# A scale's product moved to the end of its slot, and a second first product taken into the attention's last steps

## The chip, the cores and the metric

The kernel runs on one core of a Trainium2 chip. The metric is the device time of one execution in microseconds (us). Before the change three runs gave 850.76, 851.49 and 851.49 us, median 851.49 us. The rows below come from one further execution that was profiled: 851.16 us, of which the span from the first to the last instruction is 849.2 us.

## The reference

Three independent computations, all in one launch; the products have to be nearly as exact as float32.

```python
# 1: attention, 4 batches x 8 heads, 576 tokens, head size 64; heads 0-3 see a band of 32, heads 4-7 every 32nd token
attn = softmax(where(mask, q @ k.T / 8, -1e9)) @ v
# 2: x (2304 x 512), w_in (512 x 2048), w_out (2048 x 512)
h = x @ w_in
out = (h * cos(h)) @ w_out
# 3: w_gate and w_val (512 x 1536), w_out2 (1536 x 512)
out = (silu(x @ w_gate) * (x @ w_val)) @ w_out2
```

In the kernel the three are chained: the attention's output is the tokens x of the second part, whose output is the tokens of the third.

## The kernel before

**Number format.** A weight or token matrix is multiplied with a power of two (its scale, from its greatest absolute value) and split into two float16 parts: the high part on ScalarE (L272), the low part on VectorE (L275). A product of one chunk is three matmuls, high by high, high by low, low by high (L593, L594, L595). One unit of 512 tokens by 128 columns of the hidden layer is 12 matmuls of 128x512.

**Making a scale.** VectorE finds row maxima of a matrix (L201 for weights as they come from HBM, L571 for tokens), then `spread_tops` reduces them to one number for each partition (L125, then L128 and L130 or L133). `common_scale` brings that number to all partitions by a small matmul on TensorE (L140; one for each scale, up to three) and takes the maximum on VectorE (L142), followed by three tiny instructions (L117 to L119). Only then can the splits that use the scale run.

**Stages.** The attention comes first: 48 groups of scores that go through a pipeline of several steps (k = 0 to 55), with `put` (L548, L557, on ScalarE) writing the result to the token buffer at the end. In the last eight steps no new group starts. Then comes the second part in 5 blocks of tokens (512, 512, 512, 384, 384), each with 16 slots. Slot m of a block makes product m (`up1`, the 12 matmuls), and then an evaluation of h·cos(h) that is spread over this and the next slots: `up1_a` on ScalarE (L626), `up1_b` on VectorE (L629), the sine `up1_c` on ScalarE (L633; its first use loads ScalarE's function table), `up1_d` on VectorE (L636), and `up1_e` on ScalarE and GpSimd (L640, L641). The contraction with w_out (`down1`, again 12 matmuls of L593 to L595, into `acc`) runs from slot 16 on, one or two in a slot. The third part follows (L747 among its lines).

**What sets the order.** Each engine runs its instructions in the order of the program. One slot issues: the product and contractions, `up1_a` of this slot, `up1_b` of the slot before, `up1_d` and `up1_e` of earlier ones, one piece of the list `urgent` (`pump_urgent`: maxima, tops, scales and splits of the next block's tokens), and pieces of the list of weight work (`pump`: loads, maxima, splits; as many as a budget of time allows) before and after `up1_c`.

**Attention's last steps.** Where a step has no new group, TensorE gets one filler matmul of 128x384 (`keep_warm`, L827), except in two of them (k = 49, 50), where the first product of block 0 runs instead, half of its 12 matmuls in each (`EARLY = 1`). Its `up1_a` is issued in the second. The main loop then starts at slot 1. The accumulators `acc` of the main loop get the PSUM banks that the attention held, so they wait for its last `put`.

Of the kernel before, what the change touches and what calls it, by code (L numbers as in the profile page):

```python
# [30 lines left out]
LW = 64 + STRIDE  # L31
# [10 lines left out]
TX = 2.0 ** 10  # L42
# [8 lines left out]
WARM = 8  # L51
PUMP, KP = 1.05, 8
XSAT = 12
EARLY, K0 = 1, 1
HEAD, HSHARE = 16, 0.8
RATE, MINLAG = 0.7, 2
ALONE = 4
# [23 lines left out]
def build(tc, qk_l, qk_s, v_l, v_s, w_in, w_out, w_gate, w_val, w_out2, out):  # L81
    nc = tc.nc
    wide = w_in.dtype != F32
    with ExitStack() as ctx:
# [12 lines left out]
        id16 = small.tile([128, 128], BF16, name="id16")  # L97
# [359 lines left out]
        def bank():  # L457
            return pm.tile([128, 512], F32, name="bank")
# [103 lines left out]
        def scale_pieces(blks, scales, at_once=1):  # L562
            n = len(blks)
            parts = cols("parts", n * (KC + 1)).rearrange("p (n k) -> p n k", n=n)
            box = {}
            nc.gpsimd.memset(parts[:, :, KC:], TINY)
            todo = [(i, k) for i in range(n) for k in range(KC)]

            def piece(some):
                for i, k in some:  # L570
                    nc.vector.tensor_reduce(out=parts[:, i, k:k + 1], in_=xy[blks[i]][:, k, :], op=ALU.max, axis=AX.X,  # L571
                                            apply_absolute_value=True)
            for i in range(0, len(todo), at_once):
                yield 0.65 * at_once, lambda some=todo[i:i + at_once]: piece(some)
            yield 0.6, lambda: box.__setitem__("top", spread_tops(parts if n > 1 else parts[:, 0], False, n))
            yield 0.6, lambda: scales.update(zip(blks, common_scale(box["top"], TX, n)))

        def split_pieces(blk, scales, dst):
            n = BLOCKS[blk][1]
# [43 lines left out]
        def up1_a(c):  # L623
            n = c["n"]
            c["w"] = ring.tile([128, 512], F32, name="tb", bufs=4)[:, 0:n]
            nc.scalar.activation(out=c["w"].bitcast(I32), in_=c["ph"], func=AF.Identity, scale=turn[c["blk"]], bias=quarter)  # L626
# [195 lines left out]

        steps = deque()

        def keep_warm():
            t = bank()[:, 0:4 * LW].rearrange("p (n w) -> p n w", w=LW)
            nc.tensor.matmul(out=t, lhsT=id16, rhs=ml, start=True, stop=True)  # L827

        for k in range(len(gs) + LAGS[3] + 1):
            def group(lag):  # L830
                return gs[k - lag] if 0 <= k - lag < len(gs) else None
            i, g = 2 * (k // 6), k % 6
            if group(LAGS[0]):
                group(LAGS[0]).sums()
            if group(LAGS[1]):
                group(LAGS[1]).transposes()
            if group(0):
                group(0).scores()
                group(0).top()
            begun = k - len(gs) - K0  # L840
            if 0 <= begun < 2 * EARLY:
                m = begun // 2
                if begun % 2 == 0:
                    need(("in", m))
                    early = up1(0, m, range(KC // 2))
                else:
                    up1(0, m, range(KC // 2, KC), early)
                    steps.append((0, m, early))
            elif not group(0):
                keep_warm()  # L850
            if group(LAGS[3]):
                group(LAGS[3]).put()
            if group(LAGS[1]):
                group(LAGS[1]).evac()
            if group(LAGS[2]):
                group(LAGS[2]).values()
            if group(0) and g == 5:
                for j in (i + 2, i + 3):
                    if i and j < len(units):
                        load_v(j)  # L860
                for j in (i + 6, i + 7):
                    if j < len(units):
                        load_qk(j)
            if group(1):
                group(1).exps()
            if group(0):
                pump(PUMP if k >= KP else 0)
            if group(LAGS[0]):
                group(LAGS[0]).norm()
            if not group(0):  # L870
                if 0 <= begun < 2 * EARLY and begun % 2:
                    up1_a(early)
                pump(PUMP if k >= KP else 0)
            if k >= RELEASE:
                release()
# [147 lines left out]
        def urge(pieces, key=None):  # L1023
            urgent.extend((c, f, key) for c, f in pieces)

        def pump_urgent():
            if urgent:
                cost, fn, key = urgent.popleft()
                fn()
                emitted.add(key)  # L1030
                credit[0] -= cost
# [31 lines left out]
        for blk in range(NBLK):  # L1063
            for m in range(M1):
                n = BLOCKS[blk][1]
                if slot < EARLY:
                    slot += 1
                    continue
                if blk == 0:
                    need(("in", m))  # L1070
                if m == 0:
                    if blk:
                        need_urgent(("xs", blk))
                    if blk == NBLK - 1:
                        urge(fold_pieces(0, sy, ys, spans), ("ys", 0))
                if m == (2 if blk else XM) and blk + 1 < NBLK:
                    if blk == 0:
                        urge(scale_pieces([1], sx))
                    elif blk == 1:
                        urge(scale_pieces([2, 3, 4], sx, 2))  # L1080
                    urge(split_pieces(blk + 1, sx, xs), ("xs", blk + 1))
                if blk == NBLK - 2 and m == M1 // 2:
                    urge(scale_pieces([0], sy))
                if blk == NBLK - 1 and m == MINLAG + 2:
                    urge(scale_pieces([1, 2, 3], sy, 2))
                c = up1(blk, m, spare=slot // 2 % KC if slot % 2 and 1 < slot < HEAD - 4 else None)
                if blk == NBLK - 1 and m in (7, 14):
                    load_w7(m // 7 - 1)
                lag = 99 if slot < HEAD else max(MINLAG, HEAD - 2 - int((slot - HEAD) * RATE))
                work = 2.6 * n / 512  # L1090
                while len(queue) + 1 > lag:
                    work += down_next()
                if slot >= HEAD:
                    open_weights(lag)
                up1_a(c)
                up1_b(steps[-1][2])
                if len(steps) > 1:
                    up1_d(steps[-2][2])
                if len(steps) > 2:
                    finish(steps.popleft())  # L1100
                budget = (work - 1.25 * n / 512) * (HSHARE if slot < HEAD else SHARE if blk < SB else SHARE2)
                pump_urgent()
                pump(budget * 0.5)
                up1_c(steps[-1][2])
                pump(budget * 0.5)
                steps.append((blk, m, c))
                slot += 1
        up1_b(steps[2][2])
# [267 lines left out]
```

## Time and profile before

| what | value |
|---|---|
| median of three runs | 851.49 us |
| profiled execution | 851.16 us |
| its span | 849.2 us |
| TensorE busy | 841.6 us, 99% |
| VectorE busy | 650.9 us, 77% |
| ScalarE busy | 518.6 us, 61% |
| GpSimd busy | 203.1 us, 24% |
| granted TensorE clock | 1.00 |

TensorE is busy nearly all the time, so the end is set by the sum of its matmuls and of the few places where it waits. The other engines' shares are averages over stages; what matters is where one of them makes TensorE wait. The trace names at each instruction how long the engine was idle before it and what released it (in brackets). Matmuls overlap by their pipeline, so the spacing of two starts, not the duration, is what one costs.

### The profile page before, as it was taken

The page shows a single profiled execution, that of the slowest core. Times are in us where ns is not written, and L with a number is a line of the kernel's source. Part 1 is how long each engine was busy: PE and PEld are TensorE (multiplying, and loading weights), DVE is VectorE, ACT ScalarE, POOL GpSimd, SP SyncE. Part 2 cuts the span into 40 slices and gives each one's busy share as a digit, 9 for nine tenths or more (in the row PEclk, how much of TensorE's full clock was granted, in tenths as well). Part 3 has the DMA queues.
Part 4 walks back from the last instruction along what each step waited for, and adds up shares of the span by engine and source line. Part 5 has one row for each costly group of instructions (what it writes and reads, how often), then busy time and mean ns, then how long its engine had stood idle before and what let it go on. Part 6 is the DMA issues. An engine that isn't in the chain of part 4 may idle for free.

```text
span 849.2 us, 18347 instructions
## 1 busy us (share of the span) xinstructions
PE 841.6 (99%) x7225; PEld 601.0 (71%) x7225; DVE 650.9 (77%) x1256; ACT 518.6 (61%) x1047; POOL 203.1 (24%) x279
## 2 busy tenths in 40 slices
PE   9999999999999999999999999999999999999998
PEld 5677544444444444566666888888888899999998
DVE  7999988997889878799996388567756765665562
ACT  6899989555656767778985466545344444444440
POOL 5454344111445455422223001000000000000000
PEclk9999999999999999999999999999999999999999
DMA  9998812896556567415366247767777678788894
GB/s 366 408 351 304 291 62 97 304 335 252 197 199 230 194 210 223 163 49 184 113 217 237 81 183 285 249 220 263 235 252 251 231 269 293 283 304 318 323 325 162
DMA packets 53477, 201.99 MB, mean 238 GB/s; under 512 B 5264, under 2 KB 15760, under 8 KB 49552
## 3 DMA queue, kind: packets, MB, share of 16 engines
q1 hardware_dynamic: 53392, 200.84, 66.4%
q8 instruction: 56, 0.92, 0.4%
q14 instruction: 29, 0.24, 0.1%
HBM read 176.83 MB, written 23.99 MB: 236 GB/s over the span
## 4 chain that ended last, share of the span: by engine, by line
PE 81%; DVE 6%; DMA 5%; ACT 4%; POOL 1%; issue 1%; SPq 0%; ACTq 0%; POOLq 0%
PE acc L747 14%; PE bank L593 13%; PE bank L595 13%; PE bank L594 13%; PE acc L595 7%; PE acc L593 7%; PE acc L594 7%; DMA raw<-w_in 3%; PE po L535 2%; PE bank L478 2%; POOL arena L641 1%; DMA raw<-w_out 1%; ACT tb L626 1%; PE bank L747 1%; DMA raw<-w_val 1%
## 5 line engine op out<-in xcount | busy, mean ns | idle before, releaser
L593 PE MATMUL bank<-xs,wi 128*128 128x256 f16 (+3 forms) x780 | 232.6, 298 | 0.5 <-ACT cv L1244 0.5
L595 PE MATMUL bank<-xs,wi 128*128 128x256 f16 (+3 forms) x780 | 232.6, 298 | 0.0
L594 PE MATMUL bank<-xs,wi 128*128 128x256 f16 (+3 forms) x780 | 232.6, 298 | 0.0
L641 POOL TENSOR_TENSOR arena<-tb,arena 128x512 f16<-128x512 f32 (+1 forms) x80 | 89.9, 1125 | 235.3 <-ACT arena L640 202.1
L595 PE MATMUL acc<-arena 128*128 128x512 f16 (+1 forms) x320 | 114.5, 358 | 0.7 <-DVE arena L275 0.7
L593 PE MATMUL acc<-arena 128*128 128x512 f16 (+1 forms) x320 | 114.5, 358 | 0.0
L594 PE MATMUL acc<-arena 128*128 128x512 f16 (+1 forms) x320 | 114.5, 358 | 0.0
L594 PEld LDWEIGHTS <-wi 128*128 128x128 f16 x880 | 86.1, 98 | 35.8 <-issue 1.2
L593 PEld LDWEIGHTS <-wi 128*128 128x128 f16 x880 | 86.1, 98 | 34.8
L595 PEld LDWEIGHTS <-wi 128*128 128x128 f16 x880 | 86.1, 98 | 34.8
L747 PEld LDWEIGHTS <-arena 128*128 128x128 f16 x1080 | 100.8, 98 | 8.1
L731 POOL TENSOR_TENSOR wi<-tb 128x256 f32<-128x256 f32 (+1 forms) x30 | 20.2, 673 | 337.7 <-DVE tb L713 337.7
L1248 DVE TENSOR_TENSOR arena<-bank,cv 128x512 f32<-128x512 f32 (+1 forms) x60 | 37.9, 636 | 66.2 <-PE bank L595 66.2
L716 ACT ACTIVATE arena<-tb 128x256 f16<-128x256 f32 (+3 forms) x59 | 28.7, 486 | 97.1 <-DVE tb L713 90.1
L595 PEld LDWEIGHTS <-arena 128*128 128x128 f16 x600 | 58.7, 98 | 34.0 <-DVE arena L275 1.2
L594 PEld LDWEIGHTS <-arena 128*128 128x128 f16 x600 | 58.7, 98 | 32.7 <-issue 0.2
L593 PEld LDWEIGHTS <-arena 128*128 128x128 f16 x600 | 58.7, 98 | 32.4
L747 PE MATMUL acc<-arena 128*128 128x256 f16 (+1 forms) x684 | 80.2, 266 | 0.0
L640 ACT ACTIVATE arena<-tb 128x512 f16<-128x512 f32 (+1 forms) x80 | 46.6, 583 | 52.5 <-PE acc L595 50.9
L626 ACT ACTIVATE tb<-bank,quarter,c 128x512 int32<-128x512 f32 (+1 forms) x75 | 54.4, 725 | 28.9 <-PE bank L595 20.5
L713 DVE SCALAR_TENSOR_TENSOR tb<-tb,c,arena 128x512 f32<-128x512 f32 (+1 forms) x60 | 41.7, 695 | 34.4 <-ACT tb L708 34.4
L1244 ACT ACTIVATE cv<-bank 128x512 f32<-128x512 f32 (+1 forms) x90 | 49.2, 547 | 29.3 <-PE bank L595 28.4
(154 smaller groups left out, 1718.1 us busy)
## 6 DMA issues: line engine op xcount, KB each, us to landing
wi<-w SPq DMA_DIRECT2D x20, 1792.0 KB, 7.6
arena<-w SPq DMA_DIRECT2D x60, 576.0 KB, 4.8
raw<-w_out SPq DMA_DIRECT2D x56, 512.0 KB, 4.7
arena<-w SPq DMA_DIRECT2D x10, 1792.0 KB, 8.4
raw<-w_gate SPq DMA_DIRECT2D x24, 512.0 KB, 4.3
raw<-w_val SPq DMA_DIRECT2D x24, 512.0 KB, 5.6
w<-arena SPq DMA_DIRECT2D x42, 256.0 KB, 2.8
raw<-w_in SPq DMA_DIRECT2D x16, 512.0 KB, 9.1
```

The lines of the kernel that those rows point to most:

```text
L593: nc.tensor.matmul(out=o, lhsT=w[:, 0, c], rhs=x[0], start=first, stop=False, **kw)
L594: nc.tensor.matmul(out=o, lhsT=w[:, 0, c], rhs=x[1], start=False, stop=False, **kw)
L595: nc.tensor.matmul(out=o, lhsT=w[:, 1, c], rhs=x[0], start=False, stop=last, **kw)
L626: nc.scalar.activation(out=c["w"].bitcast(I32), in_=c["ph"], func=AF.Identity, scale=turn[c["blk"]], bias=quarter)
L640: nc.scalar.activation(out=g[:, 0, 0:n], in_=w, func=AF.Copy)
L641: nc.gpsimd.tensor_tensor(out=g[:, 1, 0:n], in0=w, in1=g[:, 0, 0:n], op=ALU.subtract)
L713: nc.vector.scalar_tensor_tensor(out=t, in0=t, scalar=s_g[c["blk"]], in1=c["C"][m][:, 1, 0:c["n"]], op0=ALU.mult, op1=ALU.mult)
L716: nc.scalar.activation(out=to, in_=src, func=AF.Copy, scale=2.0 ** -11)
L731: nc.gpsimd.tensor_tensor(out=t_sums[:, 0, 0:h], in0=c["t"][0][:, h:2 * h], in1=c["t"][0][:, 0:h], op=ALU.subtract)
L747: nc.tensor.matmul(out=o[:, c], lhsT=w[:, 256 * i + 128 * c:256 * i + 128 * c + 128], rhs=unit(u)[:, x:x + h], start=j == i == 0 and c == ...
L1244: nc.scalar.activation(out=t, in_=src, func=AF.Copy)
L1248: nc.vector.tensor_tensor(out=c["C"][m][:, :, h * right:h * right + h], in0=p, in1=t, op=ALU.add)
```

## The change

Two things change. `EARLY` goes from 1 to 2: the product of slot 1 of block 0 also runs in halves, at k = 51 and 52, in place of two fillers; so the fillers go from six to four, and the main loop starts at slot 2. With `up1_a` of product 1, in step 52, `up1_b` and `up1_c` of product 0 are issued too. The fillers share one PSUM bank. And the piece `common_scale` of a token scale carries a mark (`behind`): it isn't issued ahead of a slot's weight work any more, but at the slot's last place, and in the same slot as its `spread_tops`, where it used to come in the next slot. Since `up1_a`, `up1_b` and the product of that slot stand ahead, its L140 stands behind the slot's matmuls on TensorE.

```diff
-EARLY, K0 = 1, 1
+EARLY, K0 = 2, 1
...
-            yield 0.6, lambda: scales.update(zip(blks, common_scale(box["top"], TX, n)))
+
+            def spread():
+                scales.update(zip(blks, common_scale(box["top"], TX, n)))
+            spread.behind = True
+            yield 0.6, spread
...
+        warm = []
+
         def keep_warm():
-            t = bank()[:, 0:4 * LW].rearrange("p (n w) -> p n w", w=LW)
-            nc.tensor.matmul(out=t, lhsT=id16, rhs=ml, start=True, stop=True)
+            if not warm:
+                warm.append(bank()[:, 0:4 * LW].rearrange("p (n w) -> p n w", w=LW))
+            nc.tensor.matmul(out=warm[0], lhsT=id16, rhs=ml, start=True, stop=True)
...
                     up1(0, m, range(KC // 2, KC), early)
-                    steps.append((0, m, early))
...
                 if 0 <= begun < 2 * EARLY and begun % 2:
                     up1_a(early)
+                    if steps:
+                        up1_b(steps[-1][2])
+                        up1_c(steps[-1][2])
+                    steps.append((0, m, early))
...
-        def pump_urgent():
-            if urgent:
+        def pump_urgent(behind=None):
+            if urgent and behind in (None, hasattr(urgent[0][1], "behind")):
...
-                pump_urgent()
+                pump_urgent(False)
                 pump(budget * 0.5)
                 up1_c(steps[-1][2])
                 pump(budget * 0.5)
+                pump_urgent(True)
                 steps.append((blk, m, c))
```

Line numbers of the changed kernel are 4 greater from `project` on (L626 becomes L630, L629 L633, L633 L637, L636 L640).

The order of ScalarE's instructions at the end of the attention (`pt` is the last softmax block that is copied out; `xy` the token buffer that `put` writes; `wi` the parts of w_in). Before:

```order
L524 ACTIVATE pt<-tp 96x384
L272 ACTIVATE wi<-wi,s_1703 128x512
L557 ACTIVATE xy_69<-po 128x8x6
L557 ACTIVATE xy_70<-po 128x8x12
L272 ACTIVATE wi<-wi,s_1703 128x512
L548 ACTIVATE xy_70<-po 128x192
L272 ACTIVATE wi<-wi,s_1703 128x512 x2
L626 ACTIVATE tb<-bank,quarter,c_2021 128x512
L633 ACT_TABLE_LOAD
L633 ACTIVATE tb<-tb,right 128x512
```

Now:

```order
L524 ACTIVATE pt<-tp 96x384
L630 ACTIVATE tb<-bank,quarter,c_2021 128x512
L637 ACT_TABLE_LOAD
L637 ACTIVATE tb<-tb,right 128x512
L272 ACTIVATE wi<-wi,s_1703 128x512
L557 ACTIVATE xy_69<-po 128x8x6
L557 ACTIVATE xy_70<-po 128x8x12
L272 ACTIVATE wi<-wi,s_1703 128x512
L548 ACTIVATE xy_70<-po 128x192
L272 ACTIVATE wi<-wi,s_1703 128x512 x2
```

Product 1's `up1_a`, the table load and the first sine moved ahead of four high splits of w_in and of the attention's last two `put`s.

VectorE's order where the tokens of block 1 get their scale, in block 0 (`parts` are the row maxima of those tokens, `pw_out` those of w_out). Before:

```order
L125 TENSOR_REDUCE m_2316<-pw_out 128x1
L128 TENSOR_SCALAR a_2319<-m_2316 128x1
L130 SCALAR_TENSOR_TENSOR p_2317<-m_2316,a_2319 128x1
L629 SCALAR_TENSOR_TENSOR tb<-acc_2295,c_2021,tb 128x512
L636 SCALAR_TENSOR_TENSOR tb<-tb,bank 128x512
L125 TENSOR_REDUCE m_2341<-parts_2226 128x1
L133 TENSOR_SCALAR p_2342<-m_2341 128x1
L258 TENSOR_SCALAR cv<-cv 128x512
L629 SCALAR_TENSOR_TENSOR tb<-bank,c_2021,tb 128x512
L636 SCALAR_TENSOR_TENSOR tb<-tb,acc_2295 128x512
L142 TENSOR_REDUCE q_2371<-bank 128x1
```

Now:

```order
L633 SCALAR_TENSOR_TENSOR tb<-acc_2287,c_2021,tb 128x512
L640 SCALAR_TENSOR_TENSOR tb<-tb,bank 128x512
L125 TENSOR_REDUCE m_2327<-parts_2217 128x1
L133 TENSOR_SCALAR p_2328<-m_2327 128x1
L275 SCALAR_TENSOR_TENSOR wi<-wi,s_1703 128x512
L142 TENSOR_REDUCE q_2334<-bank 128x1
L117 RECIPROCAL s_2337<-q_2334 128x1
L118 TENSOR_SCALAR inv_2338<-q_2334 128x1
L119 TENSOR_SCALAR s_2337<-s_2337 128x1
```

The tokens' maximum (L142) moved up by a slot, to one instruction behind its top (L133), and ahead of w_out's top. On TensorE its L140 moved from behind product 9 to behind product 8.

The same in slot 24, where blocks 2 to 4 get theirs (`raw` holds rows of weights from HBM, `cv` a converted one, `arena` the parts of w_out). Before:

```order
L125 TENSOR_REDUCE m_3044<-parts_2620 128x3
L133 TENSOR_SCALAR p_3045<-m_3044 128x3
L201 TENSOR_REDUCE pw_two<-raw 128x1 x2
L258 TENSOR_SCALAR cv<-cv 128x512
L262 SCALAR_TENSOR_TENSOR cv<-raw,cv 128x512
L275 SCALAR_TENSOR_TENSOR arena<-cv,s_2408,arena 128x512
```

Now:

```order
L125 TENSOR_REDUCE m_3037<-parts_2607 128x3
L133 TENSOR_SCALAR p_3038<-m_3037 128x3
L142 TENSOR_REDUCE q_3043<-bank 128x3
L117 RECIPROCAL s_3048<-q_3043 128x3
L118 TENSOR_SCALAR inv_3049<-q_3043 128x3
L119 TENSOR_SCALAR s_3048<-s_3048 128x3
L201 TENSOR_REDUCE pw_two<-raw 128x1 x2
L258 TENSOR_SCALAR cv<-cv 128x512
L262 SCALAR_TENSOR_TENSOR cv<-raw,cv 128x512
L275 SCALAR_TENSOR_TENSOR arena<-cv,s_2469,arena 128x512
```

The four instructions of `common_scale` moved ahead of ten of weight work; on TensorE the three L140 moved from behind slot 25 to behind slot 24. In the same way the L140 of the first block's tokens of the third part moved from behind slot 61 to behind slot 60. The L140 of w_gate and w_val, whose piece has no mark, comes one slot later than before (behind product 27 instead of 26).

## Rows read from the trace of the kernel before

**Rows 1.** The page, busy time, share of the span and instructions.

```profile
PE 841.6 (99%) x7225; PEld 601.0 (71%) x7225; DVE 650.9 (77%) x1256; ACT 518.6 (61%) x1047; POOL 203.1 (24%) x279
```

**Rows 2.** TensorE's waits (engine, line, waited for: us, times, longest).

```profile
PE acc L595 <- DVE arena L275: 0.7, 1, 0.7
```

**Rows 3.** Timeline, TensorE, attention's end: start, us, line, out<-in, count [idle before].

```profile
93.80 0.38 PE L593 MATMUL bank<-xs,wi 128*128 128x512 f16 x1
...
95.19 0.68 PE L535 MATMUL po<-pts,v_pair 108*64 108x54 f32 x16
...
96.07 0.33 PE L827 MATMUL bank<-ml,id 128*128 128x384 bf16 x1
96.33 0.57 PE L535 MATMUL po<-pt,vl 96*64 96x64 f32 x12
...
97.19 0.33 PE L827 MATMUL bank<-ml,id 128*128 128x384 bf16 x1
...
99.04 0.38 PE L593 MATMUL bank<-xs,wi 128*128 128x512 f16 x1
...
104.22 0.38 PE L593 MATMUL acc<-xs,wi 128*128 128x512 f16 x1
```

**Rows 4.** Timeline, ScalarE, in the same stretch.

```profile
98.42 0.43 ACT L557 ACTIVATE xy<-po 128x48 f32<-128x48 f32 x2
98.64 0.73 ACT L272 ACTIVATE wi<-wi,s 128x512 f16<-128x512 f32 x1
99.25 0.34 ACT L548 ACTIVATE xy<-po 128x192 f32<-128x192 f32 x1
...
101.83 0.78 ACT L626 ACTIVATE tb<-bank,quarter,c 128x512 int32<-128x512 f32 x1 [0.51 <-PE bank L595]
102.63 1.28 ACT L633 ACT_TABLE_LOAD   x1
103.93 0.72 ACT L633 ACTIVATE tb<-tb,right 128x512 f32<-128x512 f32 x1
```

**Rows 5.** Timeline, VectorE, from there to the top of block 1's tokens.

```profile
98.56 0.75 DVE L275 SCALAR_TENSOR_TENSOR wi<-wi,s 128x512 f16<-128x512 f32 x1 [0.50 <-ACT wi L272]
...
120.30 0.15 DVE L133 TENSOR_SCALAR p<-m 128x1 int32<-128x1 int32 x1
```

**Rows 6.** Windows: busy time of each engine (instructions), clock, DMA share, GB/s.

```profile
98.56:120.45 21.89, 21.89 (x110) 10.01 (x107) 19.94 (x35) 17.49 (x29) 6.04 (x6) 1.00 0.48 174
```

**Rows 7.** Timeline, VectorE, slots 24 to 27.

```profile
194.07 1.26 DVE L201 TENSOR_REDUCE pw_two<-raw 128x1 f32<-128x512 f32 x2
...
196.31 0.74 DVE L275 SCALAR_TENSOR_TENSOR arena<-cv,s,arena 128x512 f16<-128x512 f32 x1
...
204.00 0.56 DVE L142 TENSOR_REDUCE q<-bank 128x3 f32<-128x384 f32 x1 [1.34 <-PE bank L140]
...
204.69 1.09 DVE L118 TENSOR_SCALAR inv<-q 128x3 f32<-128x3 f32 x1
...
212.97 0.15 DVE L118 TENSOR_SCALAR inv<-q 128x2 f32<-128x2 f32 x1
```

**Rows 8.** Timeline, GpSimd, beside VectorE's L118 of slot 26.

```profile
204.59 1.16 POOL L641 TENSOR_TENSOR arena<-tb,arena 128x512 f16<-128x512 f32 x1 [10.47 <-DVE q L142]
```

**Rows 9.** Timeline, TensorE, slots 25 to 27.

```profile
194.99 0.38 PE L593 MATMUL bank<-xs,wi 128*128 128x512 f16 x1
...
201.46 0.39 PE L595 MATMUL acc<-arena 128*128 128x512 f16 x1 [0.70 <-DVE arena L275]
...
203.63 0.33 PE L140 MATMUL bank<-id,p 128*128 128x128 bf16 x3
...
212.10 0.29 PE L140 MATMUL bank<-id,p 128*128 128x128 bf16 x2 [0.37 <-DVE p L130]
```

**Rows 10.** Timelines at the end of slot 60, TensorE and VectorE.

```profile
388.05 0.33 PE L593 MATMUL bank<-xs,wi 128*128 128x384 f16 x1
...
388.50 0.15 DVE L133 TENSOR_SCALAR p<-m 128x1 int32<-128x1 int32 x1
```

## The prediction

> **What bounds the kernel now.** I read the page first, then TensorE's waits, then the timelines of the places that the change touches. TensorE is busy 841.6 of 849.2 us [rows 1], and its matmuls stand back to back: from product 1 to product 3 there are 24 of them in 104.22 - 99.04 = 5.18 us, 0.216 each, 2.59 for a unit of twelve [rows 3]. The end therefore moves by what is added to or taken from TensorE's line, and by nothing else. Only two waits of the second part can be won back here. One is at 201.46, where a contraction waits for a low part of w_out from VectorE [rows 2, 9]: it is the 26th matmul after 194.99, so it was due at 200.60 and costs 0.87, of which the trace gives 0.70 as idle. The other is at 212.10, where L140 waits for the top of w_gate and w_val, 0.37 by the trace [rows 9]; with the same 0.17 that the idle time leaves out it costs 0.54. So the most that the change can give is these two and what the fillers cost. Against this stands every wait that it makes. VectorE is the engine to look at: it is busy 19.94 of 21.89 us between the attention's end and the first scale [rows 6].
>
> **Part 1, the fillers.** A filler costs 96.33 - 96.07 = 0.26 us of TensorE's line [rows 3]; two go, 0.52. The product that takes their place leaves the main loop, where it cost 2.59. In the tail a half of six matmuls takes 95.19 - 93.80 = 1.39 [rows 3], two take 2.78. So 2.78 - 2.59 - 0.52 = **-0.33 us**: product 3 could start at 103.89 instead of 104.22.
>
> **Part 2, ScalarE in the tail.** The first half now stands at 96.07 and pushes the rest by 1.39 - 0.26 = 1.13, so the second stands at 97.19 + 1.13 = 98.32 and ends at 99.71 [rows 3]. Only then can `up1_a` of product 1 run, at about 99.83; it takes 102.63 - 101.83 = 0.80 [rows 4]. The table load follows (1.30 to the next instruction), the first sine (0.62, as in the next one's start), and only then, at 102.55, what before stood ahead of it all: a high part of w_in (99.25 - 98.64 = 0.61), two `put`s of L557 (0.22), a high part (0.61), and L548 (0.34) [rows 4]. It ends at about 104.33, where before it ended at 99.59. The accumulator of product 3 lies in a bank that this `put` reads; TensorE wants it at 103.89. **+0.46 us**, between 0 (if the bank is another's) and 1.0.
>
> The load takes 1.28 us and the sine starts 0.02 after it; ahead of the load, ScalarE isn't idle either [rows 4]. The Trainium skill ("ScalarE: Activation LUTs", section "What ACT_TABLE_LOAD costs") adds a drain of about 1.38 us to a load, some 2.66 in all. By that this term would be 0.46 + 1.38 = 1.84, an estimate from that page. The rows show no drain.
>
> **Part 3, the scale of block 1's tokens.** Now L140 stands behind product 8. Before, that was the point 104.22 + 6 x 2.59 = 119.76; with parts 1 and 2 it is 119.89. It needs the top, L133, which VectorE ended at 120.30 + 0.15 = 120.45 [rows 5]. So even by the old times TensorE waits 0.6 to 0.7, where before L140 came a whole product later and found the top waiting. And VectorE is later now. Its low part at 98.56 needs the high part of ScalarE [rows 5], which by part 2 ends at 102.55 + 0.73 = 103.28. What stands between it and L133 has become less: `up1_b` of product 0 is done ahead of it (0.66), the top of w_out (three instructions, 0.46), one low part (0.66) and one row maximum (0.60) come later, together 2.38 of the 19.94 us busy [rows 6]. 103.28 + 19.94 - 2.38 = 120.84 with no idle time at all; of the 1.95 that was idle before, most was waiting for the table load, which is now over, and I leave 0.3. So the top is there at 121.15, L140 runs 0.05 later, and TensorE has waited **+1.29 us**. The bounds: 0.06 if VectorE catches up and waits no more than it must, 0.7 by the old times, and 2.9 with all of the old idle time kept. I take the sum of rows. Behind L142 on VectorE now stand the steps of products 8 and 9, and w_out's top; they have a slot's time.
>
> **Part 4, the scales of blocks 2 to 4.** L140 now stands behind slot 24, at 194.99 by the old times, and VectorE, whose line ends at 194.07, waits there for it [rows 7, 9]. Let T be the start of L140. L142 follows 204.00 - 203.63 = 0.37 later; L142, L117 and L118 take 0.69 to L118's start and 0.15 for it, as at 212.97, together 0.84 [rows 7]. Then come the two maxima and two conversions that stand before the low part at 196.31, 2.24 us, and the low part itself, 0.74 [rows 7]. That is T + 4.19. TensorE has L140 (0.16), product 25 and two matmuls of the contraction before it needs this low part: T + 3.18. Before it had 1 us to spare; now TensorE waits 1.06. The second contraction needs the next low part, five instructions on, T + 7.09 against T + 3.18 + 1.06 + 2.59 = T + 6.83: another 0.31 with the semaphore. Together 1.37, in place of the 0.87 at 201.46: **+0.50 us**. VectorE's lag from part 3 doesn't add here, for T moves with TensorE, and VectorE is early at T. The low bound is -0.87 (the low parts come from elsewhere in the order), the high one +1.44.
>
> The high one has a row: at 204.69 the same L118 took 1.09 instead of 0.15, beside an addition of GpSimd at 204.59 [rows 7, 8]. That is 0.94 more if GpSimd is at work then. Before, GpSimd was idle from 204.59 - 10.47 = 194.12 on [rows 8], so I take the short one. The Trainium skill ("GPSIMD Engine Reference", section "1. Specifications") says that GpSimd shares its interfaces to SBUF with VectorE, and names kinds of VectorE's instructions that collide with it; the rows at 204.69 and 212.97 agree, 1.09 beside 0.15.
>
> **Part 5, the scales of w_gate and w_val.** Their L140 comes one slot later, with the top long done: **-0.54 us**, safe but for what is new at that place (0 at worst).
>
> **Part 6, the third part's tokens.** Behind slot 60 TensorE is ready at 388.05, and the top is done at 388.50 + 0.15 = 388.65 [rows 10]: 0.6 us of waiting at the old times, nothing if VectorE is a little earlier against TensorE. TensorE arrives some 1.4 later by the parts before, while VectorE's steps there follow TensorE's products in part only. I take **+0.2**. The others of that kind have their tops ready before TensorE comes. At nothing I put the shared bank of the fillers, the shift of ScalarE's later steps and the queue of loads on SyncE, whose order doesn't change.
>
> **The sum.** -0.33 + 0.46 + 1.29 + 0.50 - 0.54 + 0.20 = +1.58 us on the profiled 851.16: 852.7 us. The profiled execution is 0.33 below the median of the runs, within their spread of 0.73. A measurement of this kernel can tell about 0.2% from no change, 1.7 us, that is 849.8 to 853.2; the forecast falls within it.
>
> **The rivals.**
> - *VectorE catches up.* If the low parts and the top of part 3 aren't late (the high parts of ScalarE that VectorE waits for have 19.94 of 21.89 us behind them [rows 6], but 1.95 idle), L140 costs 0.06 and the sum is 1.58 - 1.23 = +0.35: 851.5. For it speaks that the table load's wait on VectorE is gone, against it that a busy share of 91% leaves little to catch up with.
> - *Slower.* VectorE's L118 in slot 24 meets GpSimd and takes 1.09 [rows 7, 8]: TensorE waits 2.00 and not 1.06 behind slot 24, +2.52 in all, 853.7. It decides from an L118 above 0.8 on. For it: so it was where these scales stood before. Against it: GpSimd's line at 195, idle [rows 8].
> - *The lag stays.* The steps of products 9 to 17 (`up1_b`, `up1_d`) free the banks of later products; with VectorE 1.3 us behind, TensorE waits again in one or two of these slots for 0.3 to 0.6 each: +2.4 to 2.8, 853.8. Against it speaks that the waits of before show none there [rows 2].
> - *ScalarE is held longer at the table load.* If it stood still behind the load as long as the load itself takes, 1.28 [rows 4], L548 and all behind it would come so much later, and TensorE at product 3 too: +2.86, 854.0. Only the page of part 2 speaks for it; the 0.02 behind the load speaks against it.
> - *The change does only what it says.* The waits of parts 3 and 4 find cover, the two old ones go: -0.33 + 0.46 - 0.87 - 0.54 = -1.3, 849.9. It would want VectorE early in both places.
>
> **How the numbers follow.** Forecast 852.7: 0.50. VectorE catches up, 851.5: 0.18. L118, 853.7: 0.13. The lag, 853.8: 0.11. ScalarE held, 854.0: 0.03. Only gains, 849.9: 0.05. The range 850.9 to 854.3 reaches from the second to the ends of the slower cases. Slower by over 0.2% means above 853.2: the slower cases but for a little, 0.25, and a sixth of the forecast's, 0.08, together 0.33. Faster, below 849.8: half of the last, 0.03. The rest, 0.64, is within 0.2%.
>
> **What would show it.** In the profile after: product 3 waits for L548 near 104 for 0.4; L140 behind product 8 with an idle time of about 1.2 released by L133; a wait of about 1 for a low part behind product 25 and a short one in the next contraction; none at the L140 of w_gate and w_val. VectorE's L142 in slot 24 waits for L140. I am wrong if L140 behind product 8 starts without a wait, or if the wait behind product 25 is the old 0.87 or none.

## The result and the profile after

The changed kernel takes 858.33 us (median of five runs, 857.59 to 859.93), the kernel before 851.49 us beside it: 1.0084 times as long, 95% interval 1.007 to 1.0098, or +6.84 us. The forecast was 852.7 us, in a range from 850.9 to 854.3. The profiled execution has a span of 856.0 us against 849.2.

The page of the changed kernel says that TensorE still works nearly all the time and, beside [rows 1], with the same work but for two matmuls.

```profile
span 856.0 us, 18350 instructions
...
PE 842.9 (98%) x7223; PEld 600.2 (70%) x7223; DVE 658.6 (77%) x1256; ACT 520.7 (61%) x1047; POOL 205.9 (24%) x279
```

So the 6.8 us are waits. TensorE's waits of the changed kernel (engine, line, waited for: us in total, times, longest), those that answer to [rows 2]:

```profile
PE bank L140 <- DVE p L133: 2.1, 2, 1.7
...
PE bank L597 <- DVE tb L640: 1.7, 2, 1.1
PE bank L597 <- DVE q L142: 1.3, 1, 1.3
PE acc L599 <- DVE arena L275: 1.1, 2, 0.9
...
PE acc L597 <- ACT xy L548: 0.3, 1, 0.3
```

Every one but the last names VectorE. In the timeline of TensorE they stand at these places; the first row answers to the end of [rows 3], those at 203.88 and 222.42 to [rows 9], the last to [rows 10]. Where the others stand, TensorE waited for 0.14 us at most before.

```profile
104.38 0.38 PE L597 MATMUL acc<-xs,wi 128*128 128x512 f16 x1 [0.30 <-ACT xy L548]
...
121.77 0.23 PE L140 MATMUL bank<-id,p 128*128 128x128 bf16 x1 [1.69 <-DVE p L133]
...
134.79 0.22 PE L140 MATMUL bank<-id,p 128*128 128x128 bf16 x1
135.61 0.38 PE L597 MATMUL bank<-xs,wi 128*128 128x512 f16 x1 [0.60 <-DVE tb L640]
...
139.69 0.38 PE L597 MATMUL bank<-xs,wi 128*128 128x512 f16 x1 [1.33 <-DVE q L142]
...
203.88 0.39 PE L599 MATMUL acc<-arena 128*128 128x512 f16 x1 [0.94 <-DVE arena L275]
...
222.42 0.28 PE L140 MATMUL bank<-id,p 128*128 128x128 bf16 x2
...
366.95 0.32 PE L597 MATMUL bank<-xs,wi 128*128 128x384 f16 x1 [1.05 <-DVE tb L640]
...
394.79 0.23 PE L140 MATMUL bank<-id,p 128*128 128x128 bf16 x1 [0.37 <-DVE p L133]
```

The number in brackets leaves out some 0.17 us of each wait, as before. Where this text gives what a wait costs, it is the spacing of two starts less the time of the columns between them (0.216 us for 512). In this measure the two kernels compare so:

| place | before | after | foreseen change |
|---|---|---|---|
| two fillers for two half products | | -0.31 | -0.33 |
| product 3, for L548 | 0 | 0.47 | +0.46 |
| L140 behind product 8 | 0 | 1.86 | +1.29 |
| products 14 and 15, for their banks | 0 | 0.77 + 1.49 | 0 (a rival) |
| contractions and L140 of slots 24 and 25 | 0.87 | 0.13 + 0.13 + 1.11 + 0.31 | +0.50 |
| contractions of slot 26 | 0 | 0.14 + 0.35 | 0 |
| L140 of w_gate and w_val | 0.54 | 0 | -0.54 |
| product 54, for its bank | 0.14 | 1.22 | 0 |
| L140 behind slot 60 | 0 | 0.54 | +0.20 |

The changes sum to 6.7 us, and the spans differ by 6.8. So nothing is missing, and two lines that the sum had at nothing, products 14 and 15 and product 54, make half of it: 2.26 + 1.08 = 3.34.

What made products 14 and 15 wait is seen on VectorE and GpSimd. (L262 joins the two halves, `raw` and `cv`, of a weight as it comes from HBM.) VectorE:

```profile
132.65 1.65 DVE L262 SCALAR_TENSOR_TENSOR cv<-raw,cv 128x512 int32<-128x512 int32 x1
134.22 0.74 DVE L633 SCALAR_TENSOR_TENSOR tb<-acc,c,tb 128x512 f32<-128x512 f32 x1
134.88 0.67 DVE L640 SCALAR_TENSOR_TENSOR tb<-tb,bank 128x512 f32<-128x512 f32 x1
135.48 1.39 DVE L275 SCALAR_TENSOR_TENSOR xs<-xy,s,xs 128x512 f16<-128x512 f32 x1
...
138.04 1.39 DVE L275 SCALAR_TENSOR_TENSOR xs<-xy,s,xs 128x512 f16<-128x512 f32 x1
139.35 0.28 DVE L142 TENSOR_REDUCE q<-bank 128x1 f32<-128x128 f32 x1
```

GpSimd in the same stretch:

```profile
132.20 1.55 POOL L645 TENSOR_TENSOR arena<-tb,arena 128x512 f16<-128x512 f32 x1 [2.39 <-ACT arena L644]
135.16 1.16 POOL L645 TENSOR_TENSOR arena<-tb,arena 128x512 f16<-128x512 f32 x1 [1.41 <-ACT arena L644]
137.73 1.16 POOL L645 TENSOR_TENSOR arena<-tb,arena 128x512 f16<-128x512 f32 x1 [1.41 <-ACT arena L644]
```

The L140 of w_out's scale took one of the four shared PSUM banks at 134.79, and VectorE read it (L142) only at 139.35. Product 15 had to wait for that bank, product 14 for the one that `up1_d` (L640) freed at 135.55. VectorE has no idle time from 130.39 on, so it is late here (before that it had waited 1.79 us for a conversion on ScalarE). Three of its instructions take 1.39 to 1.65 us instead of 0.69 to 0.75. Each of them began while GpSimd's subtraction (L645) ran, and each ended 0.54 to 0.55 us after that subtraction did (132.65 + 1.65 = 134.30 against 133.75; 136.87 against 136.32; 139.43 against 138.89). L633 and L640, which read one operand from PSUM, keep their 0.74 and 0.67.

In the kernel before the meetings went the other way round. Between 104 and 146 us one instruction of VectorE is long, the L262 at 124.83 with 1.32 us. Three subtractions are long instead, the ones at 113.63, 130.59 and 135.95, with 1.35 to 1.65 us for the usual 1.16: each of them began while a low part or a join ran on VectorE, and VectorE's instruction kept its 0.68 to 0.75. The last of the three:

```profile
135.83 0.75 DVE L275 SCALAR_TENSOR_TENSOR arena<-cv,s,arena 128x512 f16<-128x512 f32 x1
...
135.95 1.65 POOL L641 TENSOR_TENSOR arena<-tb,arena 128x512 f16<-128x512 f32 x1 [1.41 <-ACT arena L640]
```

So in these rows the one that begins second is held up. Before the change that was mostly GpSimd, after it mostly VectorE.

### The profile page after: what moved, and what is told of

Same layout as the page of the kernel before. It is cut to its first block, busy times and chain, and to the rows that moved or that the text cites. A ratio compares the mean times of both kernels' runs of the same rounds, so it can differ in the third digit from the quotient of the medians.

```text
span 856.0 us, 18350 instructions
## 1 busy us (share of the span) xinstructions
PE 842.9 (98%) x7223; PEld 600.2 (70%) x7223; DVE 658.6 (77%) x1256; ACT 520.7 (61%) x1047; POOL 205.9 (24%) x279
## 4 chain that ended last, share of the span: by engine, by line
PE 82%; DVE 9%; DMA 3%; ACT 3%; issue 1%; SPq 0%; POOL 0%; ACTq 0%; POOLq 0%
PE acc L751 13%; PE bank L597 13%; PE bank L599 13%; PE bank L598 13%; PE acc L599 8%; PE acc L598 8%; PE acc L597 8%; DMA raw<-w_in 3%; PE po L535 2%; PE bank L478 2%; DVE tb L633 1%; DVE tb L640 1%; PE bank L751 1%; PE tp L513 1%; DVE xs L275 1%
## 5 line engine op out<-in xcount | busy, mean ns | idle before, releaser
L597 PE MATMUL bank<-xs,wi 128*128 128x256 f16 (+3 forms) x780 | 232.6, 298 | 3.5 <-DVE tb L640 1.7
L645 POOL TENSOR_TENSOR arena<-tb,arena 128x512 f16<-128x512 f32 (+1 forms) x80 | 92.2, 1154 | 239.2 <-ACT arena L644 226.3
L597 PE MATMUL acc<-arena 128*128 128x512 f16 (+1 forms) x320 | 114.5, 358 | 0.0
L597 PEld LDWEIGHTS <-wi 128*128 128x128 f16 x880 | 86.1, 98 | 34.4
L597 PEld LDWEIGHTS <-arena 128*128 128x128 f16 x600 | 58.7, 98 | 32.3 <-ACT arena L272 0.5
L630 ACT ACTIVATE tb<-bank,quarter,c 128x512 int32<-128x512 f32 (+1 forms) x75 | 54.6, 728 | 28.1 <-PE bank L599 20.0
```

Of the source, the lines that this page charges most:

```text
L597: nc.tensor.matmul(out=o, lhsT=w[:, 0, c], rhs=x[0], start=first, stop=False, **kw)
L645: nc.gpsimd.tensor_tensor(out=g[:, 1, 0:n], in0=w, in1=g[:, 0, 0:n], op=ALU.subtract)
```

## The experiments

All are built on the changed kernel unless it is said otherwise. The first four undo one part each.

**The early product alone.**

```diff
-            spread.behind = True
+
...
-                pump_urgent(True)
+
```

> The second product in the attention's last steps alone (EARLY = 2); every scale's product again in the slot after its top, as before the change. Theory (the late scales and TensorE's four shared PSUM banks make the time): what stays is -0.33 for the fillers, 0.47 at product 3, and 1.2 at product 54 (the weight work is shifted there as in the changed kernel); the waits of 1.9 behind product 8, 2.3 at products 14 and 15 and 0.5 behind slot 60 go. About 852.6 us. Rival (the table load ahead of the attention's last copies makes VectorE late, and that lag is the cost, wherever the scales stand): the waits at products 9 to 15 stay in some form, 856 us or more.

Measured: 854.93 us, 1.0049 times the kernel before (1.0033 to 1.0065). The waits behind product 8 and slot 60 are gone and the 1.20 at product 54 is there, as expected. But products 16 and 17 still wait 0.62 + 0.39, and the contraction of slot 25 waits 1.69 where before it waited 0.87. So the early product costs some 4 us by itself, and neither theory had its size right.

The waits at products 16 and 17 don't come from long instructions of VectorE: between 104 and 146 us only the low part at 109.45 is long here (1.37). L640, which frees the banks, waits for ScalarE's sine, 0.22 us for product 16 and 0.35 for product 17:

```profile
137.90 0.69 DVE L640 SCALAR_TENSOR_TENSOR tb<-tb,bank 128x512 f32<-128x512 f32 x1 [0.22 <-ACT tb L637]
```

ScalarE in turn stood 0.56 us at 132.78 for a subtraction of 1.67 us, which had begun during a low part, and has no idle time from there on to 140.8. No run takes the subtraction out of this order, so what these waits would be without it isn't known.

**The late scales alone.**

```diff
-EARLY, K0 = 2, 1
+EARLY, K0 = 1, 1
```

> The scales' products at their slot's last place alone; EARLY = 1, so the table load and the first sine stay behind the attention. Theory: the wait for the top behind product 8 is 0.6 to 0.9 instead of 1.9, none at products 14 and 15 (w_out's scale comes three slots earlier than in the changed kernel, while products still have accumulator banks to themselves), 1.1 + 0.3 instead of 0.9 behind slot 24, 0.5 behind slot 60: +1.7, 853.2 us. Rival (the place of the scales costs nothing, the early product is all): 851.5 us.

Measured: 854.71 us, 1.0043 (1.0031 to 1.0056). The wait behind product 8 is 0.75, near the 0.6 to 0.7 that the prediction read from the old times, and 1.11 + 0.31 and 0.66 (for 0.5) stand where they were expected. Not expected: 0.70 + 0.32 at products 16 and 17, though w_out's scale comes early here, and 1.24 at the L140 of w_gate and w_val (before 0.54). VectorE's rows between 124 and 146 us show what made it late ahead of the first of these; here are three of six long ones:

```profile
125.09 1.68 DVE L262 SCALAR_TENSOR_TENSOR cv<-raw,cv 128x512 int32<-128x512 int32 x1
...
127.95 1.41 DVE L275 SCALAR_TENSOR_TENSOR xs<-xy,s,xs 128x512 f16<-128x512 f32 x1
...
136.77 1.64 DVE L262 SCALAR_TENSOR_TENSOR cv<-raw,cv 128x512 int32<-128x512 int32 x1
```

In the kernel before there is one such instruction in 104 to 146 us. Here there are six of 1.39 to 1.68 us, together some 4.8 us longer than usual.

**The first sine behind the attention.**

```diff
                         up1_b(steps[-1][2])
-                        up1_c(steps[-1][2])
...
+        up1_c(steps[0][2])
         attn.close()
```

> The changed kernel, but the first sine (with the load of ScalarE's table) is issued behind the attention's last steps instead of in step 52; the rest in the same order. Theory: the 0.47 at product 3 goes, the wait behind product 8 falls from 1.9 to 0.3 to 0.9, the others (2.3, 1.1 + 0.3, 1.2, 0.5) stay: 856.8 us. Rival (VectorE's lag from the tail makes the waits at products 14 and 15 too): these go as well, 854.5 us.

Measured: 858.11 us, 1.0082 (1.0064 to 1.0099), no better than the changed kernel. The 0.47 at product 3 went, but the wait behind product 8 grew to 2.07, the 0.78 + 1.49 at products 14 and 15 stayed, and the second contraction's 0.31 became 1.09. Both theories are wrong here: VectorE's low part runs at 101.59 instead of 103.30, and yet the top is ready no earlier.

```profile
101.59 0.75 DVE L275 SCALAR_TENSOR_TENSOR wi<-wi,s 128x512 f16<-128x512 f32 x1 [2.52 <-ACT wi L272]
...
106.43 0.69 DVE L640 SCALAR_TENSOR_TENSOR tb<-tb,bank 128x512 f32<-128x512 f32 x1 [0.91 <-ACT tb L637]
...
121.65 0.15 DVE L133 TENSOR_SCALAR p<-m 128x1 int32<-128x1 int32 x1
```

The load and the sine then stand in ScalarE's way in the main loop, and VectorE waits for it there (0.91, and twice 0.38 further on). So it isn't the place of the table load that makes the top late: VectorE meets the load in either place.

**Block 1's scale at its old place.**

```diff
-            spread.behind = True
+            spread.behind = blks != [1]
...
-            if urgent and behind in (None, hasattr(urgent[0][1], "behind")):
+            if urgent and behind in (None, getattr(urgent[0][1], "behind", False)):
```

> The changed kernel, but the scale of block 1's tokens has its product in the slot after its top again; the others at their slot's last place. Theory: the 1.9 behind product 8 goes; w_out's scale comes two slots earlier, so the 2.3 at products 14 and 15 goes for the most part: 854.2 to 855 us. Rival (lag of the tail): the 1.9 turns up later, 857 us or more.

Measured: 856.19 us, 1.0059 (1.0041 to 1.0077): between the two theories. The 1.86 is gone, of the 2.26 there remain 0.65 + 0.38, at products 16 and 17, with no long instruction of VectorE but the one at 109.63, as with the early product alone; and 0.71 + 0.20 stand at 194 and 197 us, in the contraction of slot 24 and at its L140, where the changed kernel has 0.13 + 0.13. A part of the lag that was taken out at one place turned up at the next.

**GpSimd's subtraction taken out of block 0.** The first four said that the place of the scales and the early product both cost. In the changed kernel and with the late scales alone VectorE's lateness isn't explained by the order alone, since some of its instructions are long. This run takes away the second suspect, GpSimd.

```diff
-            nc.gpsimd.tensor_tensor(out=g[:, 1, 0:n], in0=w, in1=g[:, 0, 0:n], op=ALU.subtract)
+            c["blk"] and nc.gpsimd.tensor_tensor(out=g[:, 1, 0:n], in0=w, in1=g[:, 0, 0:n], op=ALU.subtract)
...
-            contract(acc_t[1, blk], wo[m], g, n, m == 0, m == M1 - 1)
+            contract(acc_t[1, blk], wo[m], g if blk else g[:, 0:1].to_broadcast([128, 2, 512]), n, m == 0, m == M1 - 1)
```

> The changed kernel without GpSimd's subtraction in block 0 (the low part of h cos h is left out there; the contraction reads the high part twice, so TensorE's work is the same). Theory (VectorE's low parts and joins of two operands in SBUF take 1.3 to 1.7 us instead of 0.7 where they meet that subtraction, and this makes VectorE late in slots 9 to 15): those instructions take 0.7 throughout, and of the waits the 0.8 and 1.5 at products 14 and 15 go, and the 1.9 behind product 8 falls by 0.5 to 1. About 855.5 us. Rival (four banks and w_out's scale in slot 12 alone): the waits at products 14 and 15 stay as they are, 858 us.

Measured: 854.56 us, 1.0036 (1.0024 to 1.0048); by the two ratios to the kernel before, 1.0084 and 1.0036, that is some 4 us less than the changed kernel; the profiled spans, 852.9 and 856.0, are 3.1 apart. The waits at products 14 and 15 are gone, and the one behind product 8 is 1.23. But for the two of 0.13 in slot 24, which are gone, everything from there on is as in the changed kernel: 1.11 + 0.31, 0.34, 1.20, 0.54. VectorE in the same place, with the same order:

```profile
121.12 0.15 DVE L133 TENSOR_SCALAR p<-m 128x1 int32<-128x1 int32 x1
...
132.21 0.68 DVE L262 SCALAR_TENSOR_TENSOR cv<-raw,cv 128x512 int32<-128x512 int32 x1
132.81 0.74 DVE L633 SCALAR_TENSOR_TENSOR tb<-acc,c,tb 128x512 f32<-128x512 f32 x1
133.47 0.67 DVE L640 SCALAR_TENSOR_TENSOR tb<-tb,bank 128x512 f32<-128x512 f32 x1
134.06 0.74 DVE L275 SCALAR_TENSOR_TENSOR xs<-xy,s,xs 128x512 f16<-128x512 f32 x1
...
136.65 0.28 DVE L142 TENSOR_REDUCE q<-bank 128x1 f32<-128x128 f32 x1
```

No instruction of two operands in SBUF is over 0.75 now, and L142 comes 2.7 us earlier. Of that, 0.97 + 0.65 + 0.65 = 2.27 are the three long instructions. The run takes away something else too: in the changed kernel ScalarE's `up1_a` waits five times for the subtraction between 104 and 146 us, 2.9 us in all. That isn't what made VectorE late ahead of L142, since VectorE didn't wait for ScalarE from 130.39 on.

**The control: the same taken out of the kernel before.**

> The kernel before with the same left out: the control. It meets the subtraction once between 122 and 146 us, and TensorE waits nowhere there, so no change beside 851 us is expected; if it gains more than 0.5 us, the subtraction costs something that the waits don't show.

Measured: 850.41 us in a single execution, beside a median of 851.22 (and a lowest of 850.68) for the kernel before. The wait of 0.87 at 201.46 is gone, the others are as before. So the subtraction of block 0 seems to cost the old order some 0.5 to 0.8 us too (the profiled spans, 848.7 and 849.2, are 0.5 apart), as much as or more than the 0.5 that was set as the limit; one execution can't settle it. In the changed order it costs 3 to 4.

**One more accumulator's bank.**

```diff
-                c = up1(blk, m, spare=slot // 2 % KC if slot % 2 and 1 < slot < HEAD - 4 else None)
+                c = up1(blk, m, spare=slot // 2 % KC if slot % 2 and 1 < slot < HEAD - 2 else None)
```

> The changed kernel, but product 13 gets an accumulator's bank too (slots 3 to 13 instead of 3 to 11), so the four shared banks carry one product less where w_out's L140 takes one. Theory of the banks: of the 0.8 + 1.5 at products 14 and 15 at most 0.8 stays, 856.8 us. Rival (VectorE is simply late by then, and each product's bank comes free late whichever it is): the waits move to products 15 and 16 with the same sum, 858 us.

Measured: 857.3 us, 1.0062 (1.0043 to 1.0081), not to be told apart from the changed kernel by its interval; the profiled spans are equal, 856.0. Both waits at products 14 and 15 are gone, so these were waits for banks. But the contractions of block 1 now wait 0.16 + 0.31 + 1.46 between 171 and 184 us for low parts of w_out, which VectorE brings late. Its waits show the exchange (the changed kernel had 1.1 in the first of these rows, and 1.7 and 1.3 for L597):

```profile
PE acc L599 <- DVE arena L275: 2.4, 3, 1.3
PE bank L140 <- DVE p L133: 2.1, 2, 1.7
...
PE bank L597 <- DVE tb L640: 1.0, 1, 1.0
```

So the lag of VectorE is the cause here, and the bank only the place where TensorE meets it first.

**The early product with its slot's weight work.** Slot 1 of the main loop used to issue 1.08 us worth of weight work. With `EARLY = 2` this slot isn't run, and all weight work comes a slot later. Here it is issued behind the attention, the scales are at their old places, and the first sine stands behind the attention too.

```diff
-            spread.behind = True
+
...
-                        up1_c(steps[-1][2])
...
-        attn.close()
+        up1_c(steps[0][2])
+        attn.close(), pump(1.08)
...
-                pump_urgent(True)
+
```

> The second product early, all scales at their old places, the first sine behind the attention, and behind it the 1.08 us worth of weight work that slot 1 used to issue, so that every engine's order from slot 2 on is that of the kernel before. Theory (the early product costs by the slot's weight work that it takes away, which shifts w_out's scale and all that follows): all waits are as before, less 0.33 for the fillers, 850.5 us against 850.8. Rival (an early product costs by itself): the waits at 138 to 142 us and at 363 us stay, 853 us or more.

Measured: 851.89 us, 1.001 (0.9994 to 1.0026): no change from the kernel before that can be told. The 1.2 at product 54 is gone (0.15), so the early product did cost by its weight work there; the place of the first sine, which is changed too, left that wait at 1.20 in the run with the late sine. But the gain of 0.33 isn't there: 0.18 at 122 and 0.57 at 138 us stand against it, and 1.21 for 0.87 in the contraction of slot 25. Between 109 and 116 us two low parts met GpSimd's subtraction (1.71 and 0.92 us), and the line of VectorE behind them is later by 0.7 than before.

**The subtraction twice, in the kernel before.**

```diff
-            nc.gpsimd.tensor_tensor(out=g[:, 1, 0:n], in0=w, in1=g[:, 0, 0:n], op=ALU.subtract)
+            [nc.gpsimd.tensor_tensor(out=g[:, 1, 0:n], in0=w, in1=g[:, 0, 0:n], op=ALU.subtract) for _ in range(1 if c["blk"] else 2)]
```

> The kernel before, with GpSimd's subtraction issued twice in block 0 (the same result). Theory (GpSimd's work beside VectorE's instructions of two operands in SBUF is what makes VectorE late there): between 104 and 146 us five or more of these take 1.3 us or more instead of one, and TensorE waits 1 to 4 us at products 13 to 16 or in the contractions up to 200 us: 852.5 to 855 us. Rival (VectorE has room there, and the changed kernel's waits come from its order alone): no wait, 851.2 us.

Measured: 867.03 us, 1.0182 (1.0161 to 1.0203), far above both. The theory's five or more instructions of 1.3 us or more aren't there: between 104 and 146 us four took 1.16 to 1.17. The run doesn't tell the two theories apart, since it opened another way: ScalarE's `up1_a` (L626) waits for GpSimd, whose subtraction still reads the buffer that `up1_a` needs. ScalarE's waits between 104 and 160 us, of this kernel and then of the kernel before:

```profile
ACT tb L626 <- POOL arena L641: 17.6, 11, 2.1
```

```profile
ACT tb L626 <- POOL arena L641: 5.0, 8, 0.8
```

TensorE's long waits in this run were followed by a lower clock (last section).

**Only the weight work shifted, in the kernel before.**

```diff
-                scale_later(TW_IN, "gate", "val")
+                later(1.0, lambda: None), scale_later(TW_IN, "gate", "val")
```

> The kernel before, with an empty piece of 1.0 us ahead of the scales of w_gate and w_val in the list of weight work, so that from slot 25 on the weight work comes some 1 us later, as in the changed kernel, and nothing else. Theory (the wait at product 54 is this shift: two low parts slip into slot 51, ahead of the steps that free the banks): 1.2 us at product 54 instead of 0.14, the 0.54 at the scales of w_gate and w_val stays: 852.3 us. Rival (it needs the late scales): 851.2 us.

Measured: 852.42 us, 1.0008 (0.9999 to 1.0018), by its time alone hardly to be told from no change; what it says is in the trace. The wait at product 54 is there with its full size, 1.21, and the 0.53 at the scales of w_gate and w_val stays; the contraction at 201 waits 1.40 instead of 0.87, which wasn't in the sum. In the trace of this kernel the two low parts that slipped in stand ahead of the top of w_out2's scale, and 1.40 us of copies behind it:

```profile
355.93 1.00 DVE L275 SCALAR_TENSOR_TENSOR xs<-xy,s,xs 128x384 f16<-128x384 f32 x1
356.86 0.87 DVE L275 SCALAR_TENSOR_TENSOR arena<-arena,s 128x256 f16<-128x256 f32 x2
...
358.10 1.40 DVE L607 TENSOR_SCALAR xy<-acc,c 128x512 f32<-128x512 f32 x2
...
361.84 0.54 DVE L636 SCALAR_TENSOR_TENSOR tb<-tb,bank 128x384 f32<-128x384 f32 x1
```

L140 of that scale has one of the four banks, so product 54 can start only when L636 has freed another, at 362.38; it starts at 362.43. A shift of 1 us in the list of background work cost 1.07 us of TensorE's line at this one place.

None of these kernels is faster than the kernel before by more than a measurement can tell.

## Why the prediction was wrong, point by point

**Part 1, the fillers: right.** Without its wait product 3 would have started at 104.38 - 0.47 = 103.91; 103.89 was foreseen.

**Part 2, ScalarE in the tail: right.** 0.47 for 0.46, the low part of VectorE at 103.30 for 103.28, and no drain behind the table load. The sine followed it at once in this trace as well:

```profile
99.84 0.78 ACT L630 ACTIVATE tb<-bank,quarter,c 128x512 int32<-128x512 f32 x1 [0.81 <-PE bank L599]
100.63 1.28 ACT L637 ACT_TABLE_LOAD   x1
101.93 0.72 ACT L637 ACTIVATE tb<-tb,right 128x512 f32<-128x512 f32 x1
```

**Part 3, L140 behind product 8: the place and the reason were right, the size low.** As foreseen, VectorE's low part waits for ScalarE until 103.30, and from there VectorE has no idle time up to the top, where the sum had left 0.3 for it. The top was ready at 121.56 + 0.15 = 121.71, not at 121.15:

```profile
103.30 0.75 DVE L275 SCALAR_TENSOR_TENSOR wi<-wi,s 128x512 f16<-128x512 f32 x1 [4.55 <-ACT wi L272]
...
109.58 1.38 DVE L275 SCALAR_TENSOR_TENSOR wi<-wi,s 128x512 f16<-128x512 f32 x1
...
121.56 0.15 DVE L133 TENSOR_SCALAR p<-m 128x1 int32<-128x1 int32 x1
```

The low part at 109.58 took 1.38 us, 0.64 more than usual; it began while GpSimd's subtraction (109.25, 1.16 us) ran. Without the subtraction the wait was 1.23 against the 1.29 of the sum. With the load moved behind the attention the wait was 2.07, and there VectorE waits for the load in the main loop.

**Behind part 3: this step failed.** "Behind L142 on VectorE now stand the steps of products 8 and 9, and w_out's top; they have a slot's time." It looked one slot ahead. What was moved out of these slots came three slots later: the L140 of w_out's scale went from behind product 10 to behind product 13, where products no longer have accumulators to themselves, and there it took one of four shared banks which VectorE, late by then, didn't read for 4.6 us. The rival "the lag stays" named the mechanism, but priced it at 0.3 to 0.6 in one or two slots and gave it 0.11; it was 0.77 + 1.49. The missing term was the stretched instructions: four in the changed kernel between 104 and 146 us, one in the kernel before. That they make this wait is shown for this order alone, by the run without the subtraction; in two other orders (the early product alone, block 1's scale at its old place) TensorE waits 1.0 us at products 16 and 17 with only one such instruction. None of the prediction's own signs of being wrong came: they looked at product 8 and slot 25, and the loss that was missed lies elsewhere.

**Part 4, blocks 2 to 4: right in its two waits.** 1.11 and 0.31 were measured for 1.06 and 0.31, L118 took 0.14, and GpSimd was indeed idle beside it (its instruction at 204.59, which the prediction calls an addition, is L641, the subtraction). Around it 0.13 + 0.13 and, in slot 26, 0.14 + 0.35 were not foreseen. The Trainium skill ("GPSIMD Engine Reference", section "1. Specifications") names VectorE's instructions with two inputs from SBUF among those that collide with GpSimd. The rows of block 0 agree, 1.38 to 1.65 us for 0.69 to 0.75. The prediction used that sentence for one tiny instruction in slot 24 and not for the low parts and joins of block 0, where it cost most.

**Part 5, w_gate and w_val: right.** Their L140 at 222.42 waits for nothing. That this depends on both parts of the change is seen from the runs with one part alone: there this L140 stays behind product 26 and waits, 0.53 with the early product, 1.24 with the late scales.

**Part 6, slot 60:** 0.54 for 0.2, within the bounds that were given, 0 and 0.6.

**At nothing, and wrong: the weight work.** With slot 1 out of the main loop, all weight work up to the third part comes about a slot later. That the list issued the same pieces in the same order was taken for no change, but which pieces fall into which slot changed. At product 54 this was 1.08 us. The run with only a shift (1.07) and the run that issued the missing work (none) show it from both sides.

How much each cause weighs can be told only roughly. By the ratios, the early product alone costs 4.2 us, the late scales alone 3.7, both together 7.2; in time they add up within their intervals, but place by place they don't, as products 14 to 17 show. Of the 7.2, 3 to 4 us go when GpSimd's subtraction is left out of block 0, against some 0.5 to 0.8 in the kernel before, so some 2 to 3 us of the change are collisions and what they set off. What stays open is why the low parts meet the subtraction in one order and not in the other: both lines shift by fractions of a microsecond, and the runs here show the meetings but no way to foresee them.

## What to carry to other kernels

Where an engine beside the critical one is nearly always busy (VectorE 91% here), follow a moved piece past the next slot: ask where everything lands that it pushes back, and which shared buffers are still plentiful there. Budget and list together decide the place of background work, so a step that is taken out of a loop takes its share of that work with it; issue the work elsewhere, as the run did that took as long as the kernel before, or put a price on the shift. And look in the trace for the same instruction with two durations: it marks a resource that the order of the instructions doesn't show.

## What the runs showed of the hardware

VectorE's low parts and joins, with both operands in SBUF (128x512, float32 or int32), took 0.68 to 0.75 us alone. Where they began during GpSimd's subtraction they took 0.89 to 1.68, and in every such case between 100 and 160 us of these traces they ended 0.54 to 0.55 us after it, so they seem to wait until it is over. The other way round it was the same: a subtraction that began with 0.15 us or more of a low part or a join still to run ended 1.01 to 1.03 us after that instruction, 1.17 to 1.72 us in all for 1.16 alone, and VectorE's kept its time. (One low part began within 0.01 us of the subtraction, in the run with the slot's weight work; there VectorE waited, 1.71 us.) With one operand in PSUM the same form kept 0.67 to 0.75. With the subtraction left out of block 0, none was long there. Two operands aren't needed for it: in the changed kernel L258, with one, took 1.39 us at 144.30, beside a subtraction from 143.91 to 145.41, and 0.43 at 130.39.

TensorE's clock fell in the run with the doubled subtraction. In the windows of that kernel (TensorE's and its weight loads' busy time, VectorE, ScalarE, GpSimd, granted clock, DMA share, GB/s) its clock is 0.61 and 0.60 behind waits of 2.83 us and 5.02 us (starts at 124.89 and 148.23); matmuls there stood 0.43 us apart, which is 1.2 GHz, and 0.216 before, which is 2.4. Behind a wait of 2.44 us, up to 216.72, they stood 0.43 apart too.

```profile
124.00:128.00 4.00, 3.11 (x9) 1.19 (x10) 0.80 (x3) 2.26 (x4) 2.51 (x3) 0.61 0.00 0
128.00:132.00 4.00, 4.00 (x20) 1.84 (x19) 3.73 (x10) 2.68 (x5) 2.52 (x3) 0.96 0.00 0
...
144.00:148.00 4.00, 0.00 (x0) 0.00 (x0) 3.29 (x5) 2.52 (x4) 2.51 (x3) 1.00 0.00 0
148.00:152.00 4.00, 3.77 (x11) 1.37 (x11) 3.62 (x7) 3.08 (x5) 2.52 (x3) 0.60 0.01 4
```

Behind the waits of 1.86 us in the changed kernel and 2.07 us in the run with the late sine the matmuls went on 0.216 apart. So a wait can cost more than its length: some eight matmuls behind each of the three long ones took 0.21 us more each.
